# Turning one group of token blocks by transposing transfers instead of TensorE, in a two-branch spectral and MLP kernel

## The chip, the cores and the metric

One Trainium2 chip, one of its cores. The metric is the device time of one execution in microseconds (us), the median of the runs shown. The profile is of one execution; its span leaves out a little at the start and the end of that execution.

The engines are called by their names or by the profile's short ones: TensorE (PE; its weight loads PEld), VectorE (DVE), ScalarE (ACT), GpSimd (POOL), and SyncE (SP), which issues the transfers. Every engine runs its instructions in the order of its own queue.

## The reference

The input is x, 2048 tokens of 448 values. Both branches work on it, and their results are added to it:

```python
x = A_x
xn = _layernorm(x, axis=-1)
return x + _A_ref(xn, A_w_r, A_w_i) + _B_ref(xn, B_w1, B_w2, B_w3, B_w4)
```

Branch A is a two-dimensional FFT of xn, a multiplication by the complex weights w_r + i w_i, and the inverse FFT. Branch B is a token mixing and an MLP:

```python
h = _gelu(_layernorm(x, axis=-1) @ w1)
...
hs = jnp.concatenate([g0, g1, g2, g3], axis=-1) @ w2
x1 = x + hs
h2 = _gelu(_layernorm(x1, axis=-1) @ w3) @ w4
return x1 + h2
```

Here g0 to g3 are the four quarters of h's columns, shifted by +1, -1, +2 and -2 tokens. w1 and w2 are 448 x 448, w3 is 448 x 1792 and w4 is 1792 x 448.

## The kernel before, in words

**Precision.** Every matmul factor is held as two 16-bit halves, hi (the value rounded) and lo (the rest), and each product is the sum of three passes, hi x hi, hi x lo and lo x hi. A "split" makes such a pair: ScalarE writes hi, VectorE then writes lo = value - hi.

**Blocks and groups.** The 2048 tokens are taken as 16 blocks; block b holds the tokens b, b + 16, b + 32 and so on, one per partition (tiles xt, 128 x 448 floats each). So a shift by one or two tokens becomes a step to a neighbouring block. `GRP` puts the blocks into four groups: group 0 is [14, 15, 0, 1], group 1 [2, 3, 4, 5], group 2 [6, 7, 8, 9] and group 3 [10, 11, 12, 13].

**First stage, by group.** `norm1(g)` normalizes the four blocks in place; for group 3 all four are done by GpSimd (lines 319 and 829). `T1(g)` (line 762) brings the group into the form that the matmuls with w1 need, with the 448 columns on the partitions: for each of four column pieces t (128, 128, 128 and 64 columns) `transpose_split` (line 363) lets TensorE transpose the piece of each of the four blocks (line 370, 32-bit, sixteen transposes a group) into one PSUM bank, and then splits the bank: ScalarE writes hi (line 374), VectorE lo (line 375), into the tile xT of the group, 128 x 7 x 512 in 16 bits. The seven planes are three hi pieces, one plane that holds the last 64 columns' hi on partitions 0 to 63 and their lo on 64 to 127, and three lo pieces. There are two buffers of xT.

`w1_unit(g, i)` (line 422) multiplies block i of the group by w1 (line 410, 11 matmuls), applies GELU on ScalarE (line 429), splits the result into hs (lines 430 and 431) and has SyncE turn it with a transposing transfer (line 434) into the tile h. Two of the five hs buffers lie in the first part of the large tile x2mem.

**Second stage, by block.** `w2_tile(b)` (line 438) adds the product of the shifted, hidden blocks and w2 to block b: 12 matmuls (line 450) and one VectorE operation (line 452). Tiles 0 to 3 need hidden blocks of groups 0 and 1, tiles 4 to 7 of groups 1 and 2 too, and tiles 8 and on those of group 3. `ln2` (line 455) is the second normalization: statistics on VectorE (line 289), centering on ScalarE and GpSimd (lines 472 and 474), the split (lines 481, 482 and 484) into a staging tile y, and a transposing transfer of each block (line 486) into x2mem. There are two staging tiles, one for each "side"; w1 and w2 were loaded into them at first.

**MLP.** `mlp` runs for pairs of blocks: a front multiplies by w3 (line 381), applies GELU and splits (lines 694 to 697); a back multiplies by w4 (line 716). Its first call, `mlp([0])`, takes blocks 0 and 1. w3 is loaded into w3raw, squared and summed for its scale (`squares`, line 238), and split by `w3_split` (lines 264 and 265, eight pieces). w4 is loaded by `load_w4(i)` in four parts (line 224: 896, 896, 672 and 672 KB) into the later part of x2mem; it too is squared (seven pieces), scaled (`powers(m4, 7, "4")`, line 863) and split into w4p.

**The order of the work.** The program is written in the order of priority. A scheduler goes through it with a model of the instructions' times, and on every engine puts first what is ready and stands earliest in the program; that fixed order is what runs. SyncE's queue is such an order as well. `behind(key)` places an instruction after the instructions that were noted under the key in the table `after`. `PIN` (line 30) names for each of the tiles 4 to 7 that its share of the splits of w3 and of the squares of w4 comes behind `"a3"`, which is group 3's last split of xT.

**Around the change** (lines 820 to 863): T1(2); behind h of group 1, the last quarter of w3 and w4's parts 0 and 1 are loaded; norm1(3); the four units of group 2; behind the last h of group 2, w4's parts 2 and 3; the squares of w3 and its scale; tiles 0 to 3, with T1(3)'s pieces 0 and 1 behind tile 1 and 2 and 3 behind tile 3; ln2 of blocks 0 and 1; tiles 4 to 7 with two splits of w3 and two squares of w4 after each; ln2 of blocks 2 and 3; the four units of group 3; w4's scale. After these come the first MLP call, the other tiles, the rest of the MLP and the FFT branch.

Of the kernel before, what the change touches and what calls it, by code (L numbers as in the profile page):

```python
# [13 lines left out]
F16 = mybir.dt.float16  # L14
I32 = mybir.dt.int32
AF = mybir.ActivationFunctionType
ALU = mybir.AluOpType
AX = mybir.AxisListType

S, D, DF, F = 2048, 448, 225, 1792  # L20
NB, NC = 16, 16
GRP = [[14, 15, 0, 1], [2, 3, 4, 5], [6, 7, 8, 9], [10, 11, 12, 13]]
# [97 lines left out]
def body(tc, nc, x, wf, w1, w2, w3, w4, c_g, c_n, c_small, out):  # L120
    V, A, P, T, SY = nc.vector, nc.scalar, nc.gpsimd, nc.tensor, nc.sync
# [13 lines left out]
    def pool(name, bufs=1, side="left", space=None):  # L135
        kw = dict(name=name, bufs=bufs, reuse_waits="tile")
        if space is not None:
            kw["space"] = space
        else:
            kw["side"] = side  # L140
        cm = tc.tile_pool(**kw)
        opened[name] = cm
        return cm.__enter__()
# [13 lines left out]
    p1 = pool("p1")  # L157
# [4 lines left out]
    def xb(b):  # L162
        return xt[b // 2][:, b % 2]
# [4 lines left out]
    def stage(name, n, side, dtype=F32):  # L168
        t = pw.tile([128, 1808], F32, tag=f"stage{side}", bufs=1, name=name)
        return (t if dtype is F32 else t.bitcast(dtype))[:, :n]  # L170
# [4 lines left out]
    def row():  # L175
        used[0] += 1
        return xr[:, 452 * (used[0] % 2):452 * (used[0] % 2) + 452]
# [41 lines left out]
    w4raw = x2mem.bitcast(F32)[:, F:].rearrange("p (f n) -> p f n", f=14)  # L219
# [3 lines left out]
    def load_w4(i):  # L223
        SY.dma_start(w4raw[:, W4F[i]:W4F[i + 1]], w4v[:, W4F[i]:W4F[i + 1]])
# [9 lines left out]
    def squares(col, src, junk=None):  # L234

        n = src.shape[-1]
        junk = xr.bitcast(F16) if junk is None else junk
        A.activation(out=junk[:src.shape[0], :n], in_=src, func=AF.Square, scale=2.0 ** -20, accum_out=col)
# [19 lines left out]
    def split_w(hi, lo, src, s, low=None):  # L258
        if low is P:
            P.tensor_scalar(out=src, in0=src, scalar1=s, scalar2=0.0, op0=ALU.mult, op1=ALU.add)  # L260
            i = A.activation(out=hi, in_=src, func=AF.Copy)
            j = P.tensor_tensor(out=lo, in0=src, in1=hi, op=ALU.subtract)
            return i.ins, j.ins
        i = A.activation(out=hi, in_=src, func=AF.Copy, scale=s)
        j = V.scalar_tensor_tensor(out=lo, in0=src, scalar=s, in1=hi, op0=ALU.mult, op1=ALU.subtract)  # L265
        return i.ins, j.ins


    def rsqrt(r, a, n, key):
        i = pc.tile([128, 8], I32, tag="ni", bufs=2, name=f"ni{key}")[:, :n]  # L270
        q = pc.tile([128, 8], F32, tag="nq", bufs=2, name=f"nq{key}")[:, :n]
        w = pc.tile([128, 8], F32, tag="nw", bufs=2, name=f"nw{key}")[:, :n]
        V.tensor_single_scalar(i, a.bitcast(I32), 1, op=ALU.logical_shift_right)
        V.tensor_scalar(out=i, in0=i, scalar1=-1, scalar2=0x5F3759DF, op0=ALU.mult, op1=ALU.add)
        y = i.bitcast(F32)
        V.tensor_tensor(out=q, in0=y, in1=y, op=ALU.mult)
        V.tensor_tensor(out=q, in0=q, in1=a, op=ALU.mult)
        V.scalar_tensor_tensor(out=q, in0=q, scalar=-10.0 / 3.0, in1=q, op0=ALU.add, op1=ALU.mult)
        V.scalar_tensor_tensor(out=w, in0=q, scalar=5.0, in1=y, op0=ALU.add, op1=ALU.mult)
        V.scalar_tensor_tensor(out=q, in0=w, scalar=-0.5 * 0.375 ** 3, in1=w, op0=ALU.mult, op1=ALU.mult)  # L280
        V.tensor_tensor(out=q, in0=q, in1=a, op=ALU.mult)
        V.scalar_tensor_tensor(out=r, in0=q, scalar=1.5 * 0.375, in1=w, op0=ALU.add, op1=ALU.mult)

    def stats(src, key, mv=None):
        if mv is None:
            mv = pc.tile([128, 4, 2], F32, tag="mv", bufs=3, name=f"mv{key}")
        for i, s in enumerate(src):
            st = pc.tile([128, 6], F32, tag="st", bufs=4, name=f"st{key}_{i}")
            V.bn_stats(out=st, in_=s)  # L289
            V.bn_aggr(out=mv[:, i, :], in_=st)  # L290
        return mv
# [61 lines left out]
    after = {}  # L353

    @contextlib.contextmanager
    def behind(*key):
        key = key if len(key) > 1 else key[0]
        with contextlib.ExitStack() as st:
            for i in after[key]:
                st.enter_context(tc.issue_after(i))  # L360
            yield
# [93 lines left out]
    def ln2(bs, engines):  # L455

        n, b0 = len(bs), bs[0]
        mv = stats([xb(b) for b in bs], f"b{b0}")
        a = pc.tile([128, 4], F32, tag="vb", bufs=2, name=f"vb{b0}")[:, :n]
        r = pc.tile([128, 4], F32, tag="vs", bufs=2, name=f"vs{b0}")[:, :n]  # L460
        o, y = [], []
        nm = pc.tile([128, 4], F32, tag="nm", bufs=2, name=f"nm{b0}")[:, :n]
        P.tensor_scalar(out=nm, in0=mv[:, :n, 0], scalar1=-1.0, scalar2=None, op0=ALU.mult)
        for m in range(0, n, 2):
            w = stage(f"y{b0 + m}", 8 * 448, (b0 + m) // 2 % 2, F16)
            o.append(w[:, 0:4 * D].bitcast(F32).rearrange("p (i n) -> p i n", i=2))
            y.append(w[:, 4 * D:8 * D].rearrange("p (i n) -> p i n", i=2))
            for i in range(2):
                e = engines[m + i]
                c = nm[:, m + i:m + i + 1]  # L470
                if e is A:
                    A.activation(out=o[-1][:, i], in_=xb(b0 + m + i), func=AF.Identity, bias=c)
                else:
                    e.tensor_scalar(out=o[-1][:, i], in0=xb(b0 + m + i), scalar1=1.0, scalar2=c,
                                    op0=ALU.mult, op1=ALU.add)
        V.tensor_scalar(out=a, in0=mv[:, :n, 1], scalar1=eps12, scalar2=None, op0=ALU.add)
        rsqrt(r, a, n, f"b{b0}")
        for i in range(n):
            b, h, x_ = b0 + i, y[i // 2][:, i % 2], o[i // 2][:, i % 2]
            k = r[:, i:i + 1]  # L480
            u = A.activation(out=h[:, 0:D], in_=x_, func=AF.Copy, scale=k)
            V.scalar_tensor_tensor(out=h[:, 448:512], in0=x_[:, 384:448], scalar=k, in1=h[:, 384:448],
                                   op0=ALU.mult, op1=ALU.subtract)
            v = V.scalar_tensor_tensor(out=h[:, 512:896], in0=x_[:, 0:384], scalar=k, in1=h[:, 0:384],
                                       op0=ALU.mult, op1=ALU.subtract)
            SY.dma_start_transpose(out=x2all[:, b // 4][:, :, 128 * (b % 4):128 * (b % 4) + 128], in_=h)
            after[f"b{b0}"] = u.ins, v.ins
# [267 lines left out]
    m1, m2, m3, m4 = (pc.tile([128, n], F32, name=f"m{i}") for i, n in ((1, 4), (2, 1), (3, 4), (4, 7)))  # L755
    junk4 = row().bitcast(F16)[:, :2 * D]
    V.memset(m1, 0.0)
    V.memset(m2, 0.0)
    xTs = {}
    flat = lambda t: t.rearrange("p a n -> p (a n)")  # L760

    def T1(g, ts=range(4)):
        if g not in xTs:
            xTs[g] = p1.tile([128, 7, 512], F16, tag="xT", bufs=2, name=f"xT{g}")
        transpose_split([xb(b) for b in GRP[g]], xTs[g], f"a{g}", ts,
                        tags=("mm", "mm", "tr", "tr") if g == 2 else ("tr", "tr", "acc", "acc"))

    def w3_split(i):
        t, cl = i % 4, slice(896 * (i // 4), 896 * (i // 4) + 896)
        split_w(w3p[:, t, cl], w3p[:, 4 + t, cl], w3raw[:, t, cl], s3)  # L770
# [49 lines left out]
    T1(2)  # L820
    with behind("h", 1, 3):
        load_w3([3])
        load_w4(0)
        load_w4(1)
    n1[2][0]()
    for n in n1:
        n[1]()
# [2 lines left out]
    h_alloc(2)  # L830
    for k in range(4):
        w1_unit(2, k)
    with behind("h", 2, 3):
        load_w4(2)
        load_w4(3)
    for k in range(4):
        with behind(*(("a2",), ("a2",), (2, 0), (2, 1))[k]):
            squares(m3[:, k:k + 1], w3raw[:, k])
# [2 lines left out]
    V.tensor_scalar(out=h3, in0=s3, scalar1=2.0 ** -5, scalar2=None, op0=ALU.mult)  # L841
    for b in range(4):
        w2_tile(b)
        if b % 2:
            T1(3, [b - 1, b])
    n1[0][0]()
    n1[0][1]()
    ln2([0, 1], [A, P])
    for b in range(4, 8):
        w2_tile(b)  # L850
        with behind(*PIN[b - 4]):
            w3_split(2 * b - 8)
            w3_split(2 * b - 7)
            for i in (2 * b - 8, 2 * b - 7):
                if i < 7:
                    squares(m4[:, i:i + 1], flat(w4raw[:, 2 * i:2 * i + 2]), junk4)
    ln2([2, 3], [A, P])
    h_alloc(3)
    for k in range(4):
# [68 lines left out]
    for n in range(17):  # L928
# [4 lines left out]
        if n:  # L933
            b = bs[n - 1]
# [30 lines left out]
```

## Time and profile before

| what | value |
|---|---|
| median of 3 runs | 420.48 us (420.2 to 420.87) |
| profiled execution | 420.4 us |
| its span | 418.6 us |
| TensorE busy | 409.8 us (98% of the span) |
| VectorE, ScalarE, GpSimd busy | 291.6, 248.1 and 118.6 us |
| granted TensorE clock | 1.00 |

Times in the profile count from the start of the span. A row of a timeline gives the start, the length, the engine, the line of the kernel, the operation and its operands (out<-in), and how many such instructions it merges. "SPq" is SyncE issuing a transfer; its length is the issue, not the transfer. A row of the grouped lines gives busy time and the mean duration in ns of one, then the engine's idle time before it. The chain of waits is followed back from the last instruction of the window; its pieces are what each step added to the end.

### The profile page before, as it was taken

Reading aid. Unit: us, or ns where it says so; the run is one execution under the profiler, and the core shown is the slowest. Engines: PE = TensorE matmul, PEld = TensorE weight load, DVE = VectorE, ACT = ScalarE, POOL = GpSimd, SP = SyncE. Lnnn points to the kernel's source line nnn. Section 1 sums busy time; section 2 is a strip of 40 time slices with the busy share of each in tenths; the row PEclk is TensorE's granted clock in tenths of the full one; section 3 lists DMA queues with packets and bytes.
Section 4 is the critical chain, followed back from the end, with each engine's and each line's share of the span. In section 5 each row is a group of like instructions: output and inputs, shape, how many; then the busy total and the mean of one; then the engine's idle time right before and its main releaser. Section 6 shows DMA issues by size and latency. Waiting matters only on the chain.

```text
span 418.6 us, 8535 instructions
## 1 busy us (share of the span) xinstructions
PE 409.8 (98%) x3329; PEld 291.7 (70%) x3329; DVE 291.6 (70%) x615; ACT 248.1 (59%) x428; POOL 118.6 (28%) x204
## 2 busy tenths in 40 slices
PE   7999999999999999999999999999999999999996
PEld 3655555765668777776887887777776767577785
DVE  4888899798774766652689889865999529942112
ACT  4698869972758866632678888864534414422331
POOL 3876700101345746300031221211454203200000
DMA  8959982734761365315056555610001003331001
GB/s 271 362 174 175 275 174 95 132 78 90 191 156 50 89 234 165 93 41 140 14 142 173 149 144 142 177 39 2 2 2 68 22 2 132 134 133 40 5 0 45
DMA packets 51832, 47.61 MB, mean 114 GB/s; under 512 B 33936, under 2 KB 47056, under 8 KB 51792
## 3 DMA queue, kind: packets, MB, share of 16 engines
q1 hardware_dynamic: 51792, 47.07, 41.7%
q8 instruction: 26, 0.43, 0.4%
q14 instruction: 14, 0.11, 0.1%
HBM read 35.52 MB, written 3.67 MB: 94 GB/s over the span
## 4 chain that ended last, share of the span: by engine, by line
PE 72%; DVE 14%; DMA 6%; issue 5%; POOL 1%; ACT 1%; SPq 1%; POOLq 0%; DVEq 0%
PE pw L381 25%; PE acc L716 22%; PE pw L450 7%; PE pw L410 6%; PE ps L536 3%; PE pu L638 2%; PE pp L593 2%; PE px L610 2%; DMA xr<-x 1%; DVE w4p L265 1%; DMA out<-xr 1%; PE pta L370 1%; DMA x2mem<-y 1%; DVE xt L682 1%; DVE sta L289 1%
## 5 line engine op out<-in xcount | busy, mean ns | idle before, releaser
L381 PE MATMUL pw<-x2mem,w3p 128*128 128x256 f16 x1232 | 151.8, 273 | 0.0
L716 PE MATMUL acc<-w4p,hf 128*128 128x448 f16 (+1 forms) x714 | 140.0, 341 | 0.7 <-DVE hf L697 0.7
L381 PEld LDWEIGHTS <-w3p 128*128 128x128 f16 x1232 | 118.9, 98 | 23.1 <-issue 0.9
L716 PEld LDWEIGHTS <-hf 128*128 128x128 f16 x714 | 69.2, 98 | 49.2 <-DVE hf L697 1.6
L697 DVE SCALAR_TENSOR_TENSOR hf<-pw,h,hf 128x512 f16<-128x512 f32 x56 | 41.7, 747 | 55.5 <-ACT hf L696 55.3
L694 ACT ACTIVATE pw<-pw,pe 128x512 f32<-128x512 f32 x56 | 36.6, 655 | 70.5 <-PE pw L381 69.4
L450 PE MATMUL pw<-w2p,h 112*128 112x448 f16 x192 | 40.1, 352 | 0.8 <-DMA h<-hs 0.8
L696 ACT ACTIVATE hf<-pw,h 128x512 f16<-128x512 f32 x56 | 38.3, 686 | 1.4
L619 POOL TENSOR_TENSOR z<-te 128x450 f32<-128x450 f32 x16 | 16.3, 1016 | 74.0 <-DVE te L617 74.0
L410 PE MATMUL pw<-w1p,xT 128*128 128x448 f16 x176 | 35.3, 352 | 0.0
L450 PEld LDWEIGHTS <-h 112*128 112x128 f16 x192 | 18.7, 98 | 17.0 <-DMA h<-hs 1.0
L666 POOL TENSOR_TENSOR e<-e 128x226 f32<-128x226 f32 x16 | 13.9, 866 | 56.5 <-ACT e L663 45.3
L410 PEld LDWEIGHTS <-xT 128*128 128x128 f16 x176 | 16.9, 98 | 16.2 <-DVE xT L375 0.8
L600 ACT ACTIVATE pf<-pp 64x450 f16<-64x450 f32 x32 | 17.3, 540 | 16.7 <-DVE pf L601 8.2
L601 DVE TENSOR_TENSOR pf<-pp,pf 64x450 f16<-64x450 f32 x32 | 19.9, 622 | 5.3 <-ACT pf L600 5.0
L663 ACT ACTIVATE e<-pe 128x452 f32<-128x452 f32 x16 | 8.7, 547 | 15.6 <-DVE vh L674 12.3
L516 POOL TENSOR_TENSOR xr<-xf 128x452 f32<-128x452 f32 x8 | 9.7, 1208 | 28.3 <-issue 22.9
L615 ACT ACTIVATE te<-px 64x450 f32<-64x450 f32 x32 | 17.2, 538 | 0.5
L673 ACT ACTIVATE vh<-e 128x448 f16<-128x448 f32 x16 | 9.2, 574 | 14.0 <-DVE e L671 8.3
L519 POOL TENSOR_TENSOR f<-xr 128x452 f32<-128x452 f32 x16 | 16.1, 1028 | 0.6
L527 DVE TENSOR_TENSOR xh<-f,xh 128x452 f16<-128x452 f32 x16 | 11.8, 780 | 5.9 <-ACT xh L526 5.9
L681 PE MATMUL py<-vh,csm 128*128 128x448 f16 x48 | 13.5, 352 | 1.5 <-DVE vh L674 0.7
(163 smaller groups left out, 602.8 us busy)
## 6 DMA issues: line engine op xcount, KB each, us to landing
wc<-wf SPq DMA_DIRECT2D x32, 225.0 KB, 3.7
wl<-wf SPq DMA_DIRECT2D x8, 450.0 KB, 3.7
xt<-x SPq DMA_DIRECT2D x8, 448.0 KB, 8.2
xf<-x SPq DMA_DIRECT2D x8, 448.0 KB, 3.7
w3raw<-w SPq DMA_DIRECT2D x3, 896.0 KB, 12.8
xr<-x SPq DMA_DIRECT2D x12, 224.0 KB, 2.6
out<-xr SPq DMA_DIRECT2D x12, 224.0 KB, 2.0
gn<-c_g SPq DMA_DIRECT2D x16, 128.0 KB, 3.3
```

Of the source, the lines that this page charges most:

```text
L381: T.matmul(ps_out, wp[:, wi + t, cols], xT[:, xi + t, tok], start=t == 0 and wi + xi == 0, stop=t == 3 and wi == 4)
L410: T.matmul(pm[:, :D], xTs[g][:, xi + t, 128 * i:128 * i + 128], w1p[:, wi + t], start=t == 0 and p == 0, stop=t == 3 and p == 2)
L450: T.matmul(pm[:, :D], hT[g][:112, 4 * hi + k, o:o + 128], w2p[:, wi, k], start=n == 0, stop=n == 11)
L519: P.tensor_tensor(out=f[:, :, k:k + 2].rearrange("p b s d -> p s b d"), in0=u[:, :, 0], in1=u[:, :, 1], op=op)
L600: A.activation(out=hi, in_=src, func=AF.Copy)
L601: V.tensor_tensor(out=lo, in0=src, in1=hi, op=ALU.subtract)
L615: A.activation(out=e[64 * h:64 * h + 64], in_=px_[64 - 64 * h:128 - 64 * h, :2 * DF], func=AF.Copy)
L619: P.tensor_tensor(out=z, in0=t[:, 0], in1=t[:, 1], op=ALU.add)
L694: A.activation(out=pm, in_=pm, func=AF.Gelu_apprx_tanh, scale=r3)
L696: i = A.activation(out=h[:, 0], in_=pm, func=AF.Copy, scale=h3)
L697: j = V.scalar_tensor_tensor(out=h[:, 1], in0=pm, scalar=h3, in1=h[:, 0], op0=ALU.mult, op1=ALU.subtract)
L716: m = T.matmul(to, h[:, hi, o:o + 128], w4p[0][:, wi, f, r], start=f == 0 and n == 0, stop=f == 13 and n == 2)
```

## The change

Group 3 is no longer transposed by TensorE. `turn(3)` takes the staging tile of side 1 as x3 and, for each block, splits the block first (ScalarE hi; VectorE lo in two pieces, of 64 and of 384 columns) into 896 columns of 16 bits, and has SyncE turn these with one transposing transfer into the block's 128 columns of all seven planes of xT. It stands behind tile 3 in the program. All four loads of w4 now stand right after it, behind the last of its transfers and behind the last h of group 2. The squares of w4 come one tile later than before, and the seventh after tile 7. The key `"a3"` now means the last split of `turn`.

```diff
+    def turn(g):
+
+        xTs[g] = p1.tile([128, 7, 512], F16, tag="xT", bufs=2, name=f"xT{g}")
+        y = stage(f"x{g}", 8 * D, 1, F16).rearrange("p (i n) -> p i n", i=4)
+        for i, b in enumerate(GRP[g]):
+            h, x_ = y[:, i], xb(b)
+            u = A.activation(out=h[:, 0:D], in_=x_, func=AF.Copy)
+            V.tensor_tensor(out=h[:, 448:512], in0=x_[:, 384:448], in1=h[:, 384:448], op=ALU.subtract)
+            v = V.tensor_tensor(out=h[:, 512:896], in0=x_[:, 0:384], in1=h[:, 0:384], op=ALU.subtract)
+            d = SY.dma_start_transpose(out=xTs[g][:, :, 128 * i:128 * i + 128], in_=h)
+        after["t", g], after[f"a{g}"] = (d.ins,), (u.ins, v.ins)
...
     with behind("h", 1, 3):
         load_w3([3])
-        load_w4(0)
-        load_w4(1)
...
-    with behind("h", 2, 3):
-        load_w4(2)
-        load_w4(3)
...
     for b in range(4):
         w2_tile(b)
-        if b % 2:
-            T1(3, [b - 1, b])
+    turn(3)
+    with behind("t", 3), behind("h", 2, 3):
+        for i in range(4):
+            load_w4(i)
     n1[0][0]()
     n1[0][1]()
     ln2([0, 1], [A, P])
...
             w3_split(2 * b - 8)
             w3_split(2 * b - 7)
-            for i in (2 * b - 8, 2 * b - 7):
-                if i < 7:
+            for i in (2 * b - 10, 2 * b - 9):
+                if i >= 0:
                     squares(m4[:, i:i + 1], flat(w4raw[:, 2 * i:2 * i + 2]), junk4)
+    squares(m4[:, 6:7], flat(w4raw[:, 12:14]), junk4)
     ln2([2, 3], [A, P])
```

## The prediction

> **What bounds the kernel now.** I read the page's engine table first, then the stages, then who made TensorE wait, then the chain of waits.
>
> ```profile
> span 418.6 us, 8535 instructions
> PE 409.8 (98%) x3329; PEld 291.7 (70%) x3329; DVE 291.6 (70%) x615; ACT 248.1 (59%) x428; POOL 118.6 (28%) x204
> ```
>
> ```profile
> 40.00:50.00 10.00, 10.00 (x56) 5.44 (x55) 8.02 (x31) 7.08 (x10) 6.45 (x20) 1.00 1.10 228
> 50.00:60.00 10.00, 10.00 (x62) 5.98 (x61) 9.94 (x30) 5.97 (x12) 1.83 (x7) 1.00 0.86 207
> 60.00:70.00 10.00, 10.00 (x54) 5.17 (x53) 9.97 (x19) 10.00 (x15) 0.00 (x0) 1.00 0.51 158
> 70.00:80.00 10.00, 10.00 (x75) 7.13 (x73) 7.18 (x23) 9.70 (x20) 1.92 (x3) 1.00 0.68 116
> ```
>
> ```profile
> PE pw L450 <- DMA h<-hs: 0.8, 1, 0.8
> PE py L681 <- DVE vh L674: 0.7, 1, 0.7
> PE acc L716 <- DVE hf L697: 0.7, 2, 0.4
> ```
>
> The rows by stage list PE, PEld, DVE, ACT and POOL busy time, then the granted clock (1.00 throughout), the DMA share and GB/s. TensorE has no idle time from 40 to 80 us, and the longest waits of it after its start are under 1 us each in the whole run. So the end is TensorE's instruction stream, and an instruction taken out of that stream is worth its own pitch, as long as the next one has its input. Beside it, VectorE is full from 50 to 70 us and ScalarE from 60 to 80 us; these are the covers that may give way.
>
> **What is removed.** The chain of waits gives each piece's share of the path (start, length, engine, line). The pieces of line 370 between 48 and 59 us are the sixteen transposes of group 3:
>
> ```profile
> 47.27 0.95 PE pw L450 x5
> 48.22 0.11 PE pta L370
> ...
> 48.90 0.11 PE pta L370
> ...
> 49.40 0.11 PE pta L370
> ...
> 50.08 0.55 PE pta L370 x5
> ...
> 55.12 0.44 PE pta L370 x4
> ...
> 58.20 0.44 PE pta L370 x4
> ...
> 73.97 5.13 PE pw L381 x47
> ```
>
> They sum to 3 x 0.11 + 0.55 + 0.44 + 0.44 = **1.76 us**, 0.11 us each, all on the path. That is the one sure term. The duration of a single transpose is longer than its pitch:
>
> ```profile
> L370 PE MATMUL pta<-ident,xt 128*128 128x128 f32 (+1 forms) x64 | 9.0, 273 | 0.0
> L374 ACT ACTIVATE xT<-pta 128x512 f16<-128x512 f32 (+1 forms) x16 | 9.0, 597 | 6.1 <-PE pta L370 6.1
> L375 DVE TENSOR_TENSOR xT<-pta,xT 128x512 f16<-128x512 f32 (+1 forms) x16 | 10.8, 684 | 2.9 <-ACT xT L374 2.8
> L481 ACT ACTIVATE y<-y,vs 128x448 f16<-128x448 f32 x16 | 9.8, 657 | 0.3
> L482 DVE SCALAR_TENSOR_TENSOR y<-y,vs 128x64 f16<-128x64 f32 x16 | 5.3, 328 | 7.3 <-ACT y L481 7.3
> L484 DVE SCALAR_TENSOR_TENSOR y<-y,vs 128x384 f16<-128x384 f32 x16 | 10.6, 665 | 0.0
> ```
>
> The 273 ns is one instruction's latency; five in a row took 0.55 us on the path, so I take the pitch. The Trainium skill, "TensorE: Matmul & The Clock Gate", Part 4 (PE-mode transpose), prices a 128x128 transpose at about 275 ns in a kernel; by that the sum would be 16 x 0.275 = 4.4 us and the time 416.0 us (an estimate). The trace agrees with that figure as a duration and not as a pitch.
>
> **What is added beside it.** ScalarE loses four evacuations of 0.597 and gets four halves from SBUF, nearest row 0.657 (L481, same shape): +0.24 us. VectorE loses 4 x 0.684 = 2.74 and gets 4 x (0.328 + 0.665) = 3.97: +1.2 us. Their other end is the pair of such instructions that ran beside GpSimd's, 1.09 and 1.35 us in the chain: 4 x 2.44 - 2.74 = +7.0 us; at the low end both are nothing. I take +1.2, because GpSimd's last large operation before that point, the normalizing of the group, is over when the halves can be made:
>
> ```profile
> 43.50 2.82 POOL L319 TENSOR_SCALAR xt<-xt,vy,nma 128x448 f32<-128x448 f32 x4
> ```
>
> ```profile
> 118.42 1.09 DVE y L482
> 119.51 1.35 DVE y L484
> ```
>
> The group's four blocks are ready one after another until 46.3 us. `turn` stands ahead of the second normalization and the splits of w3 in the program, so I expect its halves between 46 and 52 us, with those later pieces pushed back by some 2 to 4 us. That is covered: the first MLP matmul starts at 73.97 us, and of its inputs the first half of w3 is four of the eight splits that ScalarE begins here, two in 1.96 us (start, length):
>
> ```profile
> 59.17 1.96 ACT L264 ACTIVATE w3p<-w3raw,pe 128x896 f16<-128x896 f32 x2
> ```
>
> So some 10 us lie between these splits and that matmul.
>
> **What moves on SP's queue.** Columns: start, length, queue, line, operation.
>
> ```profile
> 40.03 2.20 SPq L212 DMA_DIRECT2D w3raw<-w  x2
> 42.27 1.14 SPq L224 DMA_DIRECT2D x2mem<-w  x2
> ...
> 54.34 1.22 SPq L486 DMA_TRANSPOSE x2mem<-y  x1
> 55.66 1.26 SPq L434 DMA_TRANSPOSE h<-hs  x1
> 57.02 1.26 SPq L486 DMA_TRANSPOSE x2mem<-y  x1
> 58.37 1.26 SPq L434 DMA_TRANSPOSE h<-hs  x1
> 59.69 1.13 SPq L224 DMA_DIRECT2D x2mem<-w  x2
> ```
>
> The first transpose behind the loads, by itself, and below it the issue's time to landing (us, last column), beside the median of those of y:
>
> ```profile
> 44.84 4.17 SPq L434 DMA_TRANSPOSE h<-x2mem  x1
> ```
>
> ```profile
> h<-x2mem SPq DMA_TRANSPOSE x1, 8.6
> ...
> x2mem<-y SPq DMA_TRANSPOSE x15, 3.0
> ```
>
> Behind 2 x 448 KB of w3 (the last quarter, loaded twice: 2 x 64 rows of 1792 floats) and 2 x 896 KB of w4 (4 of its 14 parts of 128 x 448 floats each), a transpose of h took 4.17 us to issue and 8.6 us to land; with the queue clear one takes about 1.26 and 3.0. After the change the first two loads of w4 (1.13 us of issue for a pair) no longer stand ahead of group 2's transposes, and four transposes of group 3 do. These cost 4 x 1.26 = 5.0 us of SP. From 44.8 us the queue then holds ten transposes (four of h, four of x, two of y): 12.6 us, until about 57.5 us if none waits, then 2.3 us for the four loads.
>
> Does TensorE have its input? From 47.27 us it has 6 x 12 = 72 matmuls of line 450 (tiles 2 to 7) at 0.19 us, 13.7 us, so until 60.9, without a single one of line 410. It needs the first turned block then at the latest, since one unit of line 410 reads one block only (before, it read four transposed pieces of all blocks). With a landing of 3.0 us the first turned block has 57.9 us as its last start; I expect 47 to 50. The other blocks come every 1.26 us against 11 x 0.19 = 2.1 us of work in each. Both bounds of this wait: nothing, or 2 us if the four transposes stand behind all of h and y. I take nothing. The last transposes of h (group 2) go no later than now for want of data, so the last tiles' slack stays at 1 to 2 us.
>
> Then the loads of w4. They start near 58 instead of 42. Of short stages, that from 62 to 64 us shows what a load does when it has the DMA engines to itself (last column, GB/s); the two rows below are the last square of w4 and the first matmul that needs its split:
>
> ```profile
> 62.00:64.00 2.00, 2.00 (x13) 1.00 (x11) 2.00 (x5) 2.00 (x4) 0.00 (x0) 1.00 1.03 387
> ```
>
> ```profile
> 81.27 0.94 ACT L238 ACTIVATE xr<-x2mem 128x896 f16<-128x896 f32 x1
> ```
>
> ```profile
> 95.46 0.54 PE L716 MATMUL acc<-w4p,hf 128*128 128x448 f16 x2
> ```
>
> 3136 KB (3.21 MB) at 387 GB/s take 8.3 us: all landed near 69. The last square of w4 runs at 81.27 now, because ScalarE is full with w3's splits before it, so the late load has some 10 us of cover; were it to land after about 80, w4's scale, its split and the first line 716 would be late one for one. I take nothing.
>
> **Sum.** 420.4 (the profiled execution, 418.6 of it span) - 1.76 + 0 = 418.64; the median of the runs is 0.08 above that execution, so **418.7 us**.
>
> **The rivals.**
> *More than the sum.* Group 2's transposes lose the loads ahead of them and w3's splits, tied to group 3's halves, may begin earlier than 59 us. All that this can free on TensorE is its idle time in between, at most the 0.8 + 0.7 + 0.7 us quoted, and most of that lies in other stages; 417.6 to 418.2. Chance 0.08.
>
> *The gain is taken back in place.* Turned blocks, or group 2's h behind them in SP's order, land 1 to 2 us after TensorE wants them, near 58 to 61 us; the same if the late halves push the hidden units' evacuations. 1.76 - (1 to 2) gives 419.7 to 420.7. For it: ten transposes in a row leave SP no gap. Against: 44 matmuls of line 410, 8.3 us, can fill for h, and tiles for x. Chance 0.20.
>
> *Slower: the y transposes behind w4.* The first MLP matmul needs the turned y of blocks 0 and 1, issued at 54.34 and 57.02 now, just ahead of w4's second half. `turn` delays the halves of y by 2 to 4 us, and the loads of w4 stand earlier in the program than y: as soon as the last transposes of x and h are out, they go. If y of block 1 is then issued behind all four loads, near 60.5, it lands behind 3.21 MB. By the full rate, 58 + 1 + 8.3 + 3.0 is about 70 us, in time for TensorE, which comes to the MLP at 73.97 - 1.76 = 72.2. By the pace of the transpose above, which landed at 44.84 + 8.6 = 53.4 behind those 2688 KB, issued from 40.03, the same 13.4 us scaled to 3136 KB make 15.6, and it lands at 74 to 76.6. TensorE would wait 1.8 to 4.4 us, so the net is 0 to +2.7: 420.5 to 423.1. It is slower from the point where y lands after 75. For it: the order of the program. Against: the slow pace before held two half-width loads of w3, and w4 alone ran at 387 GB/s. The Trainium skill, "DMA: Bandwidth & Descriptors" (Queues, rings and completion order), says that each DMA engine takes its descriptors in ring order; by that, y behind the loads waits for all of them, as the 8.6 us landing bears out. Chance 0.22.
>
> *The path is not TensorE's there*, so that taking its work out gives nothing: 420.5. With TensorE at 10.00 of 10.00 in four stages I leave 0.02 for it.
>
> **How the numbers follow.** The forecast, 418.2 to 419.6, has 0.48. A run of this kernel can tell about 0.2%, 0.84 us, from no change. Faster by that (below 419.64): the forecast's 0.48, the first rival's 0.08 and 0.02 of the second: 0.58. Within it: 0.18 of the second, 0.02 of the last and 0.04 of the slower rival's low end: 0.24. Slower (above 421.32): the slower rival's other 0.18. The range runs from the first rival's low end, 417.6, over all of the second to 421.6, which takes in the first part of the slower rival and leaves out some 0.15 above.
>
> **What the changed profile would show.** No line-370 matmul after 35 us, and sixteen fewer in all; TensorE still at 10.00 in the stages from 40 to 80 us; the first MLP matmul near 72 instead of 73.8 us; group 3's transposes on SP between 47 and 57 us, w4's four loads after them; the last square of w4 no later than 82 us and the first line-716 matmul near 93.7. The forecast is wrong if TensorE shows an idle time over 1 us between 55 and 75 us (released by a transpose of x, h or y), or near 95 us (by w4's split), or if group 3's halves run after 55 us on a full VectorE.

## The result

The change made the kernel slower by a third of a per cent: the ratio to the kernel before is 1.0034, and its 95% interval, 1.0025 to 1.0043, leaves out 1.

| kernel | median, us | runs | profiled execution's span, us |
|---|---|---|---|
| before | 420.47 (419.74 to 421.07) | 22 | 418.6 |
| changed | 422.12 (420.23 to 423.19) | 22 | 421.2 |

The range of the changed kernel is more than twice as wide. Its 22 runs fall into two sets by the mean clock that TensorE was granted: 8 runs at 0.999 or 1.000 have a mean of 420.7 us (420.2 to 421.2), 14 runs at 0.995 or 0.996 a mean of 422.5 us (421.8 to 423.2). The profiled execution is one of the 14. A mean clock lower by 0.4% over some 421 us is 1.7 us (an estimate), which is nearly all of the 1.8 us between the two sets.

The page of the changed kernel, and who made TensorE wait (the waits of over 1 us):

```profile
span 421.2 us, 8523 instructions
PE 409.6 (97%) x3313; PEld 290.4 (69%) x3313; DVE 293.5 (70%) x619; ACT 248.3 (59%) x428; POOL 119.7 (28%) x204
```

```profile
PE pw L381 <- ACT xr L238: 2.6, 1, 2.6
PE wps L752 <- DVE wsrc L183: 1.2, 1, 1.2
PE pm L245 <- DVE pt L243: 1.1, 1, 1.1
```

The first line is new: one wait of 2.6 us ahead of an MLP matmul. The timeline of TensorE shows where it is, and what follows it:

```profile
47.27 8.68 PE L450 MATMUL pw<-w2p,h 112*128 112x448 f16 x45
...
55.92 2.24 PE L410 MATMUL pw<-w1p,xT 128*128 128x448 f16 x11
...
69.36 3.00 PE L450 MATMUL pw<-w2p,h 112*128 112x448 f16 x15
74.98 7.50 PE L381 MATMUL pw<-x2mem,w3p 128*128 128x256 f16 x52 [2.61 <-ACT xr L238]
```

No line 370 stands between them any more, and TensorE has done with the tiles at 69.36 + 3.00 = 72.36 us, where before the MLP began at 73.97: 1.6 us were gained up to here. Then it idles for 2.61 us. After that, 52 matmuls of line 381 take 7.50 us; at the 47 in 5.13 us of the chain before (0.109 us each) they would take 5.7 us, or 5.8 with the full length of the last one. The stages of 1 us show why (the column after POOL is the granted clock):

```profile
74.00:75.00 1.00, 0.02 (x1) 0.05 (x2) 0.90 (x5) 0.97 (x3) 0.26 (x1) 1.00 0.43 77
75.00:76.00 1.00, 1.00 (x10) 0.89 (x11) 0.89 (x4) 0.97 (x3) 0.64 (x1) 1.00 1.28 283
76.00:77.00 1.00, 1.00 (x9) 0.74 (x7) 0.65 (x4) 0.33 (x2) 0.25 (x1) 0.62 1.26 281
77.00:78.00 1.00, 1.00 (x6) 0.73 (x5) 0.00 (x0) 0.00 (x0) 0.39 (x1) 0.50 1.12 206
78.00:79.00 1.00, 1.00 (x7) 0.72 (x5) 0.00 (x0) 0.30 (x1) 0.00 (x0) 0.50 1.08 208
79.00:80.00 1.00, 1.00 (x8) 0.77 (x7) 0.00 (x0) 1.00 (x3) 0.00 (x0) 0.68 0.33 62
```

TensorE restarts at full clock at 75, and 1.3 us later, while it is busy, the clock falls to half. The four stages from 76 to 80 lose 0.38 + 0.50 + 0.50 + 0.32 = 1.70 us of full clock, which is half clock for 3.4 us. So for this execution: -1.6 (transposes) + 2.6 (idle) + 1.7 (half clock) = +2.7 us, and the spans differ by 421.2 - 418.6 = 2.6.

What it waited for is on SyncE's queue, and the profile's "ACT xr" is not it:

```profile
48.36 5.25 SPq L777 DMA_TRANSPOSE xT<-x  x4
53.70 1.26 SPq L434 DMA_TRANSPOSE h<-x2mem  x1
56.79 1.22 SPq L486 DMA_TRANSPOSE x2mem<-y  x1
58.10 2.65 SPq L434 DMA_TRANSPOSE h<-hs  x2
60.81 2.58 SPq L224 DMA_DIRECT2D x2mem<-w  x4
63.44 10.39 SPq L486 DMA_TRANSPOSE x2mem<-y  x3
```

The first of the last three, y of block 1, alone, and the time from its issue to its landing:

```profile
63.44 5.05 SPq L486 DMA_TRANSPOSE x2mem<-y  x1
```

```profile
x2mem<-y SPq DMA_TRANSPOSE x1, 11.5
```

Issued at 63.44 behind all four loads of w4, it lands at 63.44 + 11.5 = 74.94 us, and TensorE goes on at 74.98. Before, it was issued at 57.02, ahead of w4's second half, and landed in about 3 us. Its data were ready long before: the last VectorE half of y of blocks 0 and 1 ended at 53.58 + 0.60 = 54.18 us, so it is the fixed order of the queue that held it back. The last instruction of ScalarE's line 238 that had ended by then did so at 74.17, 0.8 us before TensorE went on:

```profile
53.58 0.60 DVE L484 SCALAR_TENSOR_TENSOR y<-y,vs 128x384 f16<-128x384 f32 x1
```

```profile
73.96 0.21 ACT L238 ACTIVATION_READ_ACCUMULATOR xr<-x2mem 128x1 f32 x1
```

The releaser is only inferred from semaphores: a wait for several of them is put down to the one that came last by the profile, and where the engine named had long been done, it was another.

### The profile page after: what moved, and what is told of

The parts are those of the page before. It is cut to its first block, busy times and chain, and to the rows that moved or that the text cites. A ratio compares the mean times of both kernels' runs of the same rounds, so it can differ in the third digit from the quotient of the medians.

```text
span 421.2 us, 8523 instructions
## 1 busy us (share of the span) xinstructions
PE 409.6 (97%) x3313; PEld 290.4 (69%) x3313; DVE 293.5 (70%) x619; ACT 248.3 (59%) x428; POOL 119.7 (28%) x204
## 4 chain that ended last, share of the span: by engine, by line
PE 61%; DVE 18%; DMA 7%; issue 5%; ACT 4%; POOL 2%; SPq 1%; ACTq 0%; DVEq 0%; POOLq 0%
PE pw L381 24%; PE acc L716 22%; PE pw L410 4%; PE ps L536 3%; PE pu L638 2%; PE pp L593 2%; PE px L610 2%; DVE xt L452 1%; DMA x2mem<-y 1%; DVE hf L697 1%; DMA x2mem<-w 1%; DMA xr<-x 1%; DVE y L484 1%; DMA out<-xr 1%; DVE stb L289 1%
## 5 line engine op out<-in xcount | busy, mean ns | idle before, releaser
L381 PE MATMUL pw<-x2mem,w3p 128*128 128x256 f16 x1232 | 153.6, 274 | 2.6 <-ACT xr L238 2.6
L527 DVE TENSOR_TENSOR xh<-f,xh 128x452 f16<-128x452 f32 x16 | 13.3, 871 | 5.9 <-ACT xh L526 5.9
L463 POOL TENSOR_SCALAR nm<-mvb 128x4 f32<-128x4 f32 (+1 forms) x5 | 2.8, 559 | 43.9 <-DVE mvb L290 43.9
```

Of the source, the lines that this page charges most:

```text
L381: T.matmul(ps_out, wp[:, wi + t, cols], xT[:, xi + t, tok], start=t == 0 and wi + xi == 0, stop=t == 3 and wi == 4)
```

## The experiments

Theory A: y of block 1 waits for w4's bytes ahead of it on the queue, TensorE waits for y, and after the idle time the clock falls in most executions. Rival B: the lateness of w4 itself, its squares on ScalarE, holds TensorE, as the profile's releaser says. Rival C: turning by transfers costs more than it saves.

| run | edit | median, us | ratio to before (95%) |
|---|---|---|---|
| e1_y_first | loads of w4 behind y | 419.06 | 0.9966 (0.9954 to 0.9979) |
| e2_late_w4_only | late w4, TensorE transposes | 420.61 | 1.0003 (0.9994 to 1.0012) |
| e3_turn_only | turned, w4 as before | 421.24 | 1.0017 (1.0008 to 1.0026) |
| e5_zero_matmuls | changed, idle time filled | 420.49 | 1.0001 (0.9992 to 1.0010) |
| e6_two_ahead | two loads ahead of y | 420.12 | 0.9990 (0.9981 to 0.9999) |
| e7_three_ahead | three loads ahead of y | 419.93 | 0.9986 (0.9977 to 0.9995) |
| e4_no_squares | changed, no squares of w4 | 420.15 | 0.9997 (0.9985 to 1.0010) |
| e8_fold_later | e1, first fold later | 417.87 | 0.9939 (0.9926 to 0.9952) |
| e9_fold_alone | before, first fold later | 419.95 | 0.9982 (0.9973 to 0.9991) |

### y ahead of the loads

```diff
-    with behind("t", 3), behind("h", 2, 3):
-        for i in range(4):
-            load_w4(i)
...
     ln2([0, 1], [A, P])
+    with behind("t", 3), behind("h", 2, 3), behind("y", 1):
+        for i in range(4):
+            load_w4(i)
```

(ln2 notes its transfer under `("y", b)`.)

> Theory A: the four loads of w4 stand ahead of the turned y of block 1 on SP's queue, and TensorE waits for it (2.6 us, then a lower granted clock). Here only this order is changed: the loads come behind y of block 1. A: no idle time of TensorE near 72 us, clock 1.00, the sixteen transposes' 1.76 us are gained, 418.3 to 419.4 us. Theory B: the late w4 itself (its squares on ScalarE, which the profile names as the releaser) holds TensorE: w4 is 1.3 us later still, so 422 us or more. Theory C: the turning itself costs more than it saves: about 422 us.

Measured: 419.06 us. SyncE's queue and TensorE, in the profiled execution:

```profile
57.85 2.66 SPq L434 DMA_TRANSPOSE h<-hs  x2
60.56 1.30 SPq L486 DMA_TRANSPOSE x2mem<-y  x1
61.91 2.45 SPq L224 DMA_DIRECT2D x2mem<-w  x4
```

```profile
71.58 1.30 PE L450 MATMUL pw<-w2p,h 112*128 112x448 f16 x6
72.72 5.08 PE L381 MATMUL pw<-x2mem,w3p 128*128 128x256 f16 x45
```

The order of this one transfer and the four loads is all that was swapped on the queue. y, issued at 60.56, lands in 3.1 us; w4 comes 1.1 us later still; TensorE has no idle time here, and 45 matmuls take 5.08 us, which is full pace. (The scheduler also put seven MLP matmuls among the last matmuls of the tiles.) B and C fall. Of the 1.76 us, 1.40 arrive in the median; the wait list shows what took back a part, a wait for hf of 1.23 us that was 0.38 us before:

```profile
PE acc L717 <- DVE hf L698: 1.4, 2, 1.2
```

### Each part alone

Late w4 only:

```diff
     for b in range(4):
         w2_tile(b)
-    turn(3)
-    with behind("t", 3), behind("h", 2, 3):
+        if b % 2:
+            T1(3, [b - 1, b])
+    with behind("h", 2, 3):
         for i in range(4):
             load_w4(i)
```

> Group 3 is transposed by TensorE as before; all four loads of w4 come behind the last h of group 2. On SP's queue y of blocks 0 and 1 then stand ahead of the loads. A: no wait, 420.2 to 421.0 us, as before. B: late w4 alone costs, 421.5 to 423 us. C: 420.5 us.

420.61 us, no difference. With no `turn` in front, both y are ready before the last h, and they stand ahead of the loads:

```profile
55.60 1.26 SPq L486 DMA_TRANSPOSE x2mem<-y  x1
56.95 1.26 SPq L434 DMA_TRANSPOSE h<-hs  x1
58.27 2.57 SPq L224 DMA_DIRECT2D x2mem<-w  x4
```

So late loads cost nothing that these runs can tell. They go out at 58.27 here, 2.5 us earlier than in the changed kernel; the run above, with 61.91, covers that. The other part, `turn` with the loads (and squares) of w4 at their places of before:

```diff
     with behind("h", 1, 3):
         load_w3([3])
+        load_w4(0)
+        load_w4(1)
...
         w1_unit(2, k)
+    with behind("h", 2, 3):
+        load_w4(2)
+        load_w4(3)
...
     turn(3)
-    with behind("t", 3), behind("h", 2, 3):
-        for i in range(4):
-            load_w4(i)
```

> Group 3 is turned by transfers; the loads and the squares of w4 stand where they stood before the change. Only 1344 KB of w4 (its second half) stand ahead of y of block 1. A: by 387 GB/s y lands some 4.5 us earlier than 74.9 us in the changed kernel, that is before TensorE wants it at 72: 418.5 to 419.6 us. B: 418.7 us too. C: about 422 us.

421.24 us, above what A and B expected. By C one would have said "the turning costs"; the waits say which:

```profile
PE pw L450 <- DMA h<-x2mem: 1.4, 1, 1.4
PE pw L450 <- DMA h<-hs: 1.2, 2, 0.8
```

```profile
49.27 7.12 SPq L777 DMA_TRANSPOSE xT<-x  x4
56.48 1.26 SPq L434 DMA_TRANSPOSE h<-x2mem  x1
```

w4's first half is ahead of the turned blocks; their four transfers take 7.12 us to issue instead of 5.25, and h of group 2 behind them starts at 56.48 instead of 53.70 (49.55 in the kernel before). TensorE waits 2.6 us for h, 1.8 more than before, which is the whole gain in the profiled execution. That one took 420.56 us, the least of the 11; the 0.7 us that the median has above it are not explained by this trace. So moving w4's first half back was needed for `turn` to pay; it went too far by one transfer.

### Does the clock count by itself?

```diff
                 n += 1
+            if (b, n) == (9, 6):
+                for _ in range(14):
+                    T.matmul(pm[:, :D], wsrc[:, 0:128], wsrc[:, :D], start=False, stop=False)
```

> The changed kernel, with fourteen matmuls of zeros added into the accumulation of tile 9, at the place where TensorE waits (14 x 0.19 = 2.65 us of work for 2.61 us of idle time). If the lower granted clock after the idle time is a cost of its own (52 matmuls of line 381 in 7.50 us instead of 5.8), the clock stays at 1.00 and the time is 420.47 - 1.76 + 2.6 = 421.3 us, with the spread of before. If only the wait counts, 422.1 us with the wide spread of the changed kernel. If the wait is short in most executions, the zeros cost: 423 us or more.

420.49 us (420.37 to 421.45): 1.6 us less than the changed kernel, by adding work. All 11 runs have a clock of 0.999 or 1.000, and in the profiled execution the MLP goes on behind the zeros without a wait:

```profile
72.19 2.81 PE L454 MATMUL pw<-wsrc 128*128 128x448 f16 x14
74.84 3.22 PE L381 MATMUL pw<-x2mem,w3p 128*128 128x256 f16 x28
```

28 matmuls in 3.22 us are full pace. The median is 0.8 us below the 421.3 expected. The zeros take their 2.6 us in every execution, so the sum should hold for all; the profiled one, at 421.45 the slowest of the 11, agrees with it, and what the others gain is not shown. The scheduler also put the later MLP matmuls in a somewhat different order. So this run shows that with the idle time filled the clock stays up; what a lower clock costs is read from the two sets of runs of the changed kernel, and of the kernel without squares below.

### How many bytes ahead

Two loads ahead of y, and the others behind it (with three ahead, `range(3)` and the fourth alone):

```diff
     with behind("t", 3), behind("h", 2, 3):
-        for i in range(4):
+        for i in range(2):
             load_w4(i)
...
     ln2([0, 1], [A, P])
+    with behind("y", 1):
+        for i in range(2, 4):
+            load_w4(i)
```

> Two of the four loads of w4 (1792 KB) are issued ahead of y of block 1, two behind it. Theory A (y waits for the bytes ahead of it): y landed at 74.94 us behind 3.21 MB; 1.38 MB less at 380 GB/s is 3.6 us earlier, 71.3 us, before TensorE comes at about 72: no idle time, 419.0 to 419.4 us, as with y ahead of all. Theory B (late w4 costs): no better than the changed kernel, 422 us.

> Three of the four loads (2464 KB) ahead of y of block 1, the fourth behind it. A: y lands 0.69 MB, 1.8 us, earlier than 74.94, at 73.1: an idle time of about 0.9 us, too short for the clock, so 419.1 + 0.9 = 420.0 us (419.6 to 420.4). B: 422 us.

Measured 420.12 and 419.93 us. Time from issue to landing of y with two loads ahead, and TensorE:

```profile
x2mem<-y SPq DMA_TRANSPOSE x1, 8.5
```

```profile
70.45 0.38 PE L381 MATMUL pw<-x2mem,w3p 128*128 128x256 f16 x2 [1.18 <-DMA x2mem<-y]
70.67 1.87 PE L450 MATMUL pw<-w2p,h 112*128 112x448 f16 x9
```

The same with three:

```profile
x2mem<-y SPq DMA_TRANSPOSE x1, 9.6
```

```profile
72.18 0.92 PE L381 MATMUL pw<-x2mem,w3p 128*128 128x256 f16 x7 [1.08 <-DMA x2mem<-y]
```

y was issued at 61.80 and 62.46, so it lands at 70.3 and 72.1, and at 74.9 with four loads ahead: the third load, of 0.69 MB, moves it by 1.8 us and the fourth by 2.8, and y ahead of all lands at 60.56 + 3.1 = 63.7. The bytes of one such load alone take 1.8 us at 380 GB/s; what the fourth adds to that is not explained. This bears A out. With two loads I expected no wait and there is one of 1.18: the scheduler, expecting y earlier, had put two MLP matmuls ahead of nine of a tile, and TensorE asked for y at 69.3 and not at 72. Here the profile also names the transfer as the releaser. None of these 22 runs shows a clock below 0.999, with waits of 1.1 to 1.2 us in the two profiled executions.

### The releaser that the profile named

The squares of w4 are left out of the changed kernel (so its w4 is scaled by another power of two).

```diff
-            for i in (2 * b - 10, 2 * b - 9):
-                if i >= 0:
-                    squares(m4[:, i:i + 1], flat(w4raw[:, 2 * i:2 * i + 2]), junk4)
-    squares(m4[:, 6:7], flat(w4raw[:, 12:14]), junk4)
+    V.memset(m4, 1.0)
```

> The changed kernel with the squares of w4 left out (its scale is then worked out from ones). If TensorE waited for ScalarE's squares, as the profile names them as the releaser, the idle time near 72 us is gone: 418.5 to 419.5 us. A: y still stands behind all four loads, the idle time of 2 to 2.6 us stays, and with it the lower clock in most executions: 420.5 to 422.5 us.

The wait is still there, now with nobody named; y takes 10.5 us to land:

```profile
PE pw L381 <- issue: 1.7, 1, 1.7
```

```profile
x2mem<-y SPq DMA_TRANSPOSE x1, 10.5
```

So the squares were not what TensorE waited for, and it goes on at 73.92 as y lands, at 63.33 + 10.5 = 73.83. The wait is 0.9 us shorter than in the changed kernel, as y lands 1.1 us earlier; why it does is not shown. The time, 420.15 us, lies between the two ranges. Nine of 11 runs are at full clock, with a median of 420.06 us, two at 0.995, with 422.14 and 421.97. Here, with a wait of 1.7 us in the profiled execution, the clock fell in 2 of 11 runs; in the changed kernel, with one of 2.6, in 14 of 22. The runs with the lower clock are 1.8 us (changed kernel) and 2.0 us (here) longer.

### A version faster than both

```diff
-FOLD = [(0, 5), (1, 0), ...
+FOLD = [(0, 6), (1, 0), ...
```

on top of y ahead of the loads, and then on the kernel before alone:

> The kernel with y ahead of w4, and the first fold of the FFT branch placed one front later, behind front 6 of the first MLP call instead of front 5. In the kernel with y ahead, a wait of TensorE for hf of 1.23 us (0.38 before) took back part of the gain; on VectorE ahead of that hf stand y's halves, slowed beside GpSimd's fold (1.09 and 1.43 us instead of 0.28 and 0.61). If the fold sets that wait, it falls to nothing and the time to 418.0 to 418.6 us; if the y of the last blocks sets it, 419.1 us.

> The kernel before, with nothing changed but the first fold of the FFT branch placed behind front 6 instead of front 5. It parts the 2.6 us of the kernel with y ahead and the fold later into its two halves. If the fold only takes away the wait that the earlier TensorE had run into (1.23 us, of which 0.38 was there before), it gives 0.3 to 0.5 us here: 420.0 to 420.2 us. If placing the fold later is worth more by itself, 419.3 us or less, and the rest, about 1.5 us, is what turning group 3 by transfers gains.

417.87 and 419.95 us. The wait of 1.23 us for hf is gone (TensorE has 2.00 of 2.00 in each stage of 2 us from 116 to 124), and y's halves are no longer slowed: with y ahead alone, the fourth pair took 1.09 and 1.43 us while GpSimd folded, and with the fold later

```profile
115.53 0.28 DVE L482 SCALAR_TENSOR_TENSOR y<-y,vs 128x64 f16<-128x64 f32 x1
115.73 0.61 DVE L484 SCALAR_TENSOR_TENSOR y<-y,vs 128x384 f16<-128x384 f32 x1
```

The fold alone gives 0.0018 of 420.6, about 0.75 us (0.4 to 1.1 by the interval), a little more than the 0.3 to 0.5 that its wait would explain. The rest of the 0.0061, 0.0043 or 1.8 us, is what turning gains with both waits out of the way, if the two gains simply add up. The two intervals together leave some 0.7 us on either side; it agrees with the 1.76 us of the prediction.

## Why the prediction was wrong

**What is removed: right.** 1.76 us of TensorE's stream; 1.6 us showed up at the place, and 1.8 us, give or take 0.7, at the end once the two waits were out of the way (e8 against e9).

**What is added beside it: right.** The halves of x ran from 46.9 to 51.6 us, as forecast from the end of the normalization. VectorE's pieces took 0.23 and 0.55 us, shorter than the rows used; no wait of TensorE came of them. The halves of y were pushed back by 1.4 us (the last one ended at 54.18 instead of 52.83), less than the 2 to 4 us expected.

**TensorE's input from the turned blocks: right.** The first turned block was issued at 48.36; no wait of lines 410 or 450 was added.

**w4's lateness: right.** Its last square began at 80.41 (81.27 before), and e2 shows no cost.

**The y transposes: the step that failed.** The prediction named the mechanism, with its place, its price and the point from which it decides, gave it 0.22, and took the low end of two bounds: y "by the full rate, 58 + 1 + 8.3 + 3.0 is about 70 us, in time for TensorE". The 0 that stands for this rival in the sum was the term that failed: TensorE waited 2.6 us for y. The full rate was right, the start of it was not:

```profile
60.00:62.00 2.00, 2.00 (x13) 0.99 (x11) 2.00 (x4) 2.00 (x3) 0.00 (x0) 1.00 1.04 192
62.00:64.00 2.00, 2.00 (x12) 1.04 (x11) 2.00 (x5) 2.00 (x3) 0.00 (x0) 1.00 0.90 223
64.00:66.00 2.00, 2.00 (x13) 1.02 (x11) 2.00 (x3) 2.00 (x3) 0.00 (x0) 1.00 1.02 371
66.00:68.00 2.00, 2.00 (x12) 1.04 (x11) 2.00 (x3) 1.95 (x5) 0.00 (x0) 1.00 1.06 401
```

The loads were issued at 60.81 and not at 58, because the queue did wait ("until about 57.5 us if none waits"). h of block 7 came behind the four transfers of x, at 53.70 instead of the 49.55 of before:

```profile
49.55 2.84 SPq L434 DMA_TRANSPOSE h<-x2mem  x1
```

The first y had to wait for that h to land, since both use the same part of x2mem. Then the two transposes of h just ahead of the loads kept the DMA engines until about 62.6 (59.42 + 3.2), and the loads moved at full rate (371 to 401 GB/s) only from about 63.2, where the estimate had 58 + 1. That is 2.8 us from the late issue and 1.4 us from the h ahead. With the prediction's own terms, 63.2 + 8.3 + 3.0 is 74.5; the last 0.4 us to 74.9 are not placed. The rate was bounded from two rows; the start of the queue was an estimate without a bound, and the range of this rival should have been worked out from the latest start, not from both ends of the rate. The 74 to 76.6 of its upper end takes in the 74.9, but by a slower rate, which is not what happened.

**The clock: a term that was missing.** The prediction read the clock as 1.00 throughout and priced an idle time at its own length. Here the half clock after an idle time of 2.6 us cost another 1.7 us, and that lifted the median out of the range: the 8 runs without it have a mean of 420.7 us, which is within 0.2% of before and near the low end of that rival's 420.5 to 423.1. The Trainium skill, "TensorE: Matmul & The Clock Gate", Part 1 (What's actually happening), states half clock after at least one idle window and full clock after a busy one, each of about 3.4 us, with windows that run free of the kernel. The trace agrees with the half clock (0.50) and with its length (3.4 us), and that it came in 14 of 22 runs fits windows that run free. It differs in that 2.6 us of idle time, shorter than that window, were enough. Why they were is not shown.

**The other rivals.** The gain taken back by h and x late in the queue did not happen in the changed kernel, but it is what happened in e3, with w4's first half at its old place. "More than the sum" did not happen.

## What to carry to other kernels

- When transfers change their order on one queue, list for the whole queue what stands ahead of the next transfer on the critical path, in bytes and in waits: a transpose of 224 KB that lands in 3 us took 11.5 behind 3.2 MB, and swapping it with those loads turned +0.34% into -0.34%.
- Where TensorE is full, a wait of it can have two prices, its length (2.6 us here) and what the clock does after it (1.7 us). A kernel whose runs spread more than twice as wide as before is worth splitting by granted clock before anything is explained.
- Two parts of a change can each be useless alone (e2, e3) and be worth something together, once the order between them is right (e1), so undoing one part at a time can mislead without the wait lists beside it.

## What was not expected of the hardware

- The clock fell 1.3 us after TensorE had restarted, not during the idle time: at 75 to 76 us it was still 1.00, from 77 to 79 it was 0.50.
- Idle times of 1.1 to 1.2 us went with no lower clock in 22 runs, one of 1.7 us with 2 of 11 runs at a lower clock, and one of 2.6 us with 14 of 22 (each idle time as the profiled execution has it).
- Fourteen matmuls of zeros in the place of an idle time made the changed kernel 1.6 us faster; all 11 runs had a clock of at least 0.999.
